# Placing the finest level's sums: half tiles of TensorE replaced by quarter tiles, twice as many

## The chip, the cores and the metric

The kernel runs on one core of one Trainium2 chip. The metric is the device time of one execution in microseconds, as the median of several runs. Beside it there is one profiled execution, whose trace gives every instruction's start and duration; its span is the time from its first to its last instruction. Both are given below.

## The reference

Two blocks follow each other. The first is a recurrent attention (RWKV6) with batch 4, 8 heads, 768 tokens and 48 channels a head; the second is a feed-forward layer with an exact GELU on the 3072 rows of 384 that come out of it.

```python
for t in range(S):
    kt, vt, rt, wt = (k[:, :, t], v[:, :, t], r[:, :, t], w[:, :, t])
    cur = np.einsum('bhd,bhe->bhde', u[None] * kt, vt)
    y[:, :, t] = np.einsum('bhd,bhde->bhe', rt, state + cur)
    state = wt[:, :, :, None] * state + np.einsum('bhd,bhe->bhde', kt, vt)
...
h = x @ w_in
g = 0.5 * h * (1.0 + erf(h / sqrt(2)))
out = g @ w_out
```

In chunks of 64 tokens the recurrence becomes a matrix of weights A between the tokens of a chunk (how much token i counts for the later token j: the sum over the channels of k, r and all decays w between them), times v, plus a term from the state before the chunk. All is 32-bit floating point.

## The kernel before

The work is cut into eight pieces x = 0 to 7 (batch element times half of the 768 tokens: 384 tokens each, C = 64 to a chunk). In a piece there are 4 pairs of heads. The two heads of a pair (g = 0, 1) lie in partitions 0 to 63 and 64 to 127 (48 of 64 rows are used). The six chunks of a pair are taken two at a time (p = 0, 1), so there are n_b = 12 units of two chunks of two heads in a piece. `a_sb` holds A: its partitions are the 128 tokens of the unit's two chunks, its columns the 64 tokens of the same chunk, for both heads and all 12 units.

Pieces 0 and 1 build A in `halves()` (line 492), by levels of doubling size. Pieces 2 to 7, six in all, build it in `quarters()` (line 563), by two levels of a factor of four, h = FINE = 4 and h = 16 (`QUARTERS`, loop at line 592), and what is finer than 4 tokens, the finest level, apart. The finest level is this: VectorE multiplies k and r token by token for all pairs of tokens (distance e = 0 to 3) within groups of four (`apart`, line 405, and line 414), and one VectorE instruction for each distance (`transposed_sums`, line 400) transposes them in blocks of 32 by 32 and adds them up over 32 channels. `fine_sb[row, e, a, n]` then holds, in row 32z + i, what the block z of 32 channels adds to the pair of tokens (4i + a, 4i + a + e) of unit n. Two such blocks z belong to a head.

What is left is to add the two blocks of a head and to bring the sum for token 4i + a to row 4i + a. TensorE does both, with `places` (made once, lines 304 to 309): a matrix of zeros and ones whose row 32z + i has its one in column 4i + a. Line 601 multiplies, for each a = 0 to 3 and each head g, the 64 rows of head g of `places` (stationary, 128 columns, hence a half tile of the array: 64 rows by 128 columns) by (4 - a) times 12 columns of `fine_sb` (48, 36, 24 and 12 columns), and adds the products up in the last 48 columns of the bank of PSUM that belongs to g (`fine_of`, line 615). That is 8 products a piece.

These products stand in `burst` (line 595), which issues the level's main products: line 609 multiplies, for each unit n, head g and chunk p, a 64 by 64 block of k by 96 columns of r laid out in `kx` (a quarter tile of the array: 64 rows by 64 columns). For h = FINE there are three bursts of 5, 5 and 2 units. The last one (`behind == n_b`) issues the 8 placing products first and then its own 8. Then come, on VectorE, line 663 (r of the next level), line 670 and line 674 (k of the next level, which may start only once the last burst has read k), lines 585 and 586 (laying out), the copies of the burst's blocks to `a_sb` under masks (line 642), and at last two masked copies of the finest level's sums from PSUM to `a_sb` (line 692), one for each head. ScalarE copies plain parts of r to `kx` (line 580) after the last burst. The level h = 16 repeats this without the finest level; in pieces 2, 3, 5 and 7 it issues its bursts in one go, and two tiles named `d` of two banks each go around between all bursts, so its first burst or its second waits until line 692 has read the tile of FINE's last burst. Later in a piece, lines 732 (k times v), 773 (A times v) and 818 (state times r) are quarter tiles too, with 48 and 64 columns.

All engines work through their queues in the order in which the program issues; no scheduler changes it. The order between the pieces is written by hand: `PLAN[x]` is a string in which each letter advances one stream by one step up to its next `yield`: "." the feed-forward layer of piece x - 1 (`mlp`, products at lines 950, 1076, 1090 and 1222 with full tiles of 128 by 128), "s" the attention of piece x, and others for loads and sums. So the bursts of piece x stand in TensorE's queue between the big products of piece x - 1, and ScalarE's GELUs and copies and VectorE's sums for that layer stand between the attention's steps.

In the trace every 32-bit product shows as two passes, each with a weight load (LDWEIGHTS) and a matmul (MATMUL) of its own.

Of the kernel before, what the change touches and what calls it, by code (L numbers as in the profile page):

```python
# [20 lines left out]
C = 64  # L21
# [9 lines left out]
FINE = 4  # L31
# [44 lines left out]
def kernel(  # L76
# [25 lines left out]
    nc = tc.nc  # L102
# [21 lines left out]
    def pair(name):  # L124
        return pools["d"].tile([128, 2, BANK], F32, name=name, tag="d")
# [9 lines left out]
    def bank_u(i):  # L135
        return pools["u"].tile([128, BANK], F32, name="u_ps", tag=f"u{i % 2}")
# [5 lines left out]
    half = [slice(0, 64), slice(64, 128)]  # L142
# [14 lines left out]
    fine_sb = bufs[0][:, SPARE:SPARE + FINE * FINE * NPART * NI].rearrange("p (e a n) -> p e a n", e=FINE, a=FINE)  # L157
    places = bufs[0][:, 3 * ALL - FINE * 128:].rearrange("p (a r) -> p a r", a=FINE)
# [217 lines left out]
    def attention(x, unit):  # L376
# [186 lines left out]
        def quarters():  # L563
# [27 lines left out]
            n_b = np_ * NI  # L591
            for h in QUARTERS:
                m, r4, t4, s0, s1, s2 = views(h)

                def burst(first, behind, spare=False):

                    d = [bank_u(i) for i in range(2)] if spare else pair("d")
                    if behind == n_b and h == FINE:
                        for a in range(FINE):
                            for g in range(2):  # L600
                                nc.tensor.matmul(fine_of(d, g)[:, a * n_b:], lhsT=places[half[g], a],  # L601
                                                 rhs=fine_sb[half[g], 0:FINE - a, a],
                                                 start=(a == 0), stop=True, skip_group_check=True)
                    for n in range(first, behind):
                        i = n - first
                        for g in range(2):
                            for p in range(2):
                                o = d[g] if isinstance(d, list) else d[:, g]
                                nc.tensor.matmul(o[half[p], i * 3 * C // 2:(i + 1) * 3 * C // 2],  # L609
                                                 lhsT=kc[half[g], n // NI, n % NI, p],  # L610
                                                 rhs=rx[half[g], 2 * n + p], start=not spare or i == 0, stop=True,
                                                 skip_group_check=True)
                    return d

                def fine_of(d, g):
                    return d[:, g, BANK - FINE * n_b:]
# [30 lines left out]
                cuts = (0, n_b // 3, 2 * n_b // 3, n_b) if whole else (0, 5, 10, n_b)  # L647
                parts_of = list(zip(cuts, cuts[1:]))
                ds = [burst(*parts_of[0])]
                if not whole:  # L650
                    yield
                ds.append(burst(*parts_of[1]))
                if whole:
                    ds.append(burst(*parts_of[2], spare=True))
# [67 lines left out]
        def vs(b, i, g):  # L722
            o = ((parts[b] * NI + i) * 2 + g) * D
            return loaded[x][1][:, o:o + G]

        kvs = []
        for b in range(np_):
            kv_ps = pair("kv_ps")
            for i in range(NI):
                for p in range(2):  # L730
                    for g in range(2):
                        nc.tensor.matmul(kv_ps[half[g], p, i * D:(i + 1) * D], lhsT=k_t(b, i, p, g),  # L732
                                         rhs=vs(b, i, g)[half[p], 0:D], start=True, stop=True)
# [74 lines left out]
        for i in range(NI):  # L808
            for p in range(2):
                for b in range(np_):  # L810
                    q, c3 = divmod(i, N3)
                    for g in range(2):
                        c = 2 * c3 + (p + g) % 2
                        src, c0 = (st, c - 1) if c else (before, NC - 1)
                        if src is None:
# [3 lines left out]
                                         lhsT=src[half[g], o:o + G], rhs=rc[half[g], b, i, c % 2],  # L819
                                         start=False, stop=True, skip_group_check=True)  # L820
# [525 lines left out]
```

## Time and profile before

| | |
|---|---|
| median of 3 runs | 598.23 us (598.77, 595.89, 598.23) |
| profiled execution, its own time | 597.41 us |
| its span | 595.6 us |
| TensorE clock granted, mean | 0.997 |
| passes of line 601 in the trace | 96, of 256 to 307 ns each as the profile models them |
| passes of line 609 in the trace | 1152, of 242 to 294 ns each |

The profile's durations of matmuls overlap: they are pipelined, and their ends are modelled. What a group of products costs TensorE is read from where it starts and where the next group starts. "PE" is TensorE's matmuls, "PEld" its weight loads, "DVE" VectorE, "ACT" ScalarE. A form such as 64*128 64x48 is a tile of 64 rows by 128 columns and a moving operand of 48 columns. In a timeline line the columns are the start in us from the span's start, how long the merged group lasts, the engine, the line of the kernel, the operation, what it writes and reads, and how many records it merges; in brackets, how long the engine had been idle and for whom it waited.

### The profile page before, as it was taken

Reading aid. Unit: us, or ns where it says so; the run is one execution under the profiler, and the core shown is the slowest. Engines: PE = TensorE matmul, PEld = TensorE weight load, DVE = VectorE, ACT = ScalarE, POOL = GpSimd, SP = SyncE. Lnnn points to the kernel's source line nnn. Section 1 sums busy time; section 2 is a strip of 40 time slices with the busy share of each in tenths; the row PEclk is TensorE's granted clock in tenths of the full one; section 3 lists DMA queues with packets and bytes.
Section 4 is the critical chain, followed back from the end, with each engine's and each line's share of the span. In section 5 each row is a group of like instructions: output and inputs, shape, how many; then the busy total and the mean of one; then the engine's idle time right before and its main releaser. Section 6 shows DMA issues by size and latency. Waiting matters only on the chain.

```text
span 595.6 us, 17175 instructions
## 1 busy us (share of the span) xinstructions
PE 577.2 (97%) x7410; PEld 511.3 (86%) x7424; DVE 447.2 (75%) x857; ACT 280.0 (47%) x647; POOL 8.0 (1%) x21
## 2 busy tenths in 40 slices
PE   5779999999999999999999999999999999999997
PEld 3566666656699999999999999999999999999997
DVE  5978989997868977798849977799858978631211
ACT  2258789313533645235652554335652454435500
POOL 3100000000000000000000000000000000000000
PEclk8999999999999999999999999999999999999999
DMA  7467753220141301431032310432022100310000
GB/s 235 137 221 284 263 180 110 75 69 1 19 131 49 125 2 18 127 120 38 1 63 89 106 50 8 115 103 76 3 40 79 62 1 2 68 32 0 1 14 27
DMA packets 50859, 46.79 MB, mean 79 GB/s; under 512 B 31712, under 2 KB 35936, under 8 KB 50784
## 3 DMA queue, kind: packets, MB, share of 16 engines
q1 hardware_dynamic: 50688, 45.62, 25.1%
q8 instruction: 58, 0.95, 0.6%
q14 instruction: 17, 0.14, 0.1%
q10 hardware_dynamic: 96, 0.07, 0.1%
HBM read 36.24 MB, written 4.72 MB: 69 GB/s over the span
## 4 chain that ended last, share of the span: by engine, by line
PE 92%; DMA 2%; DVE 2%; ACT 1%; issue 1%; SPq 0%; DVEq 0%; ACTq 0%
PE o_ps L1090 31%; PE h_ps L950 16%; PE u_ps L950 13%; PE h_ps L1076 10%; PE o_ps L1222 5%; PE d L609 4%; PE kv_ps L732 2%; PE y_ps L773 2%; PE y_ps L818 2%; PE d L475 2%; PE u_ps L1090 2%; DMA raw<-in_w_in_dram 1%; DMA rkw<-in_rkw_dram 1%; PE d L601 1%; DVE rkw L528 0%
## 5 line engine op out<-in xcount | busy, mean ns | idle before, releaser
L950 PE MATMUL h_ps<-xT,w_in_sb 128*128 128x192 f32 x480 | 95.0, 330 | 0.0
L950 PEld LDWEIGHTS h_ps<-xT,w_in_sb 128*128 128x128 f32 x480 | 79.7, 190 | 3.1 <-ACT g L982 1.4
L1076 PE MATMUL h_ps<-xT,w_in_sb 128*128 128x384 f32 x192 | 64.2, 490 | 0.4 <-ACT g L1079 0.4
L1076 PEld LDWEIGHTS h_ps<-xT,w_in_sb 128*128 128x128 f32 x192 | 35.8, 190 | 24.2 <-ACT g L1079 0.5
L1090 PE MATMUL o_ps<-w_out_sb,g 128*128 128x192 f32 x224 | 39.7, 326 | 0.0
L1090 PEld LDWEIGHTS o_ps<-w_out_sb,g 128*128 128x128 f32 x224 | 37.0, 190 | 0.3
L950 PE MATMUL u_ps<-s,w_in_sb 128*128 128x192 f32 x192 | 35.1, 326 | 0.0
L475 PEld LDWEIGHTS d<-rkw 64*64 64x64 f32 x1152 | 19.1, 137 | 15.6 <-issue 8.6
L1222 PE MATMUL o_ps<-w_out_sb,g 128*128 128x384 f32 x96 | 32.5, 491 | 0.0
L625 ACT COPY a_sb<-d 32x256 f32<-32x256 f32 (+8 forms) x84 | 30.5, 363 | 3.4 <-PE d L609 2.0
L642 DVE COPY_PREDICATED a_sb<-quarter,d 128x480 f32<-128x480 uint8 (+5 forms) x54 | 23.1, 438 | 11.9 <-PE d L609 10.6
L950 PEld LDWEIGHTS u_ps<-s,w_in_sb 128*128 128x128 f32 x192 | 31.9, 190 | 0.0
L1150 DVE TENSOR_TENSOR u<-o_ps,p 128x192 f32<-128x192 f32 x7 | 2.5, 357 | 37.3 <-PE o_ps L1090 37.3
L1090 PE MATMUL o_ps<-w_out_sb,f 128*128 128x192 f32 x160 | 29.4, 331 | 0.0
L747 DVE SCALAR_TENSOR_TENSOR st<-st,tot_sb,kv_ps 128x48 f32<-128x48 f32 x160 | 28.8, 256 | 0.2 <-PE kv_ps L732 0.2
L475 PE MATMUL d<-rkw 64*64 64x64 f32 (+1 forms) x1152 | 21.5, 224 | 7.7 <-DMA rkw<-in_rkw_dram 3.7
L1090 PE MATMUL o_ps<-t,g 128*128 128x192 f32 x160 | 28.6, 330 | 0.0
L1004 DVE TENSOR_TENSOR g<-g,o_sb 128x384 f32<-128x384 f32 x24 | 13.1, 547 | 20.4 <-ACT o_sb L986 20.4
L1090 PE MATMUL o_ps<-w_out_sb,e 128*128 128x192 f32 x160 | 28.4, 329 | 0.0
L1090 PE MATMUL o_ps<-t,e 128*128 128x192 f32 x160 | 28.0, 327 | 0.0
L1090 PE MATMUL o_ps<-t,s 128*128 128x192 f32 x160 | 27.7, 327 | 0.0
L1222 PEld LDWEIGHTS o_ps<-w_out_sb,g 128*128 128x128 f32 x96 | 17.7, 190 | 11.4
(170 smaller groups left out, 1195.2 us busy)
## 6 DMA issues: line engine op xcount, KB each, us to landing
rkw<-in_rkw_dram SPq DMA_DIRECT2D x54, 256.0 KB, 3.7
raw<-in_w_out_dram SPq DMA_DIRECT2D x8, 768.0 KB, 4.5
v_in<-in_v_dram SPq DMA_DIRECT2D x8, 584.0 KB, 4.3
raw<-in_w_in_dram SPq DMA_DIRECT2D x5, 768.0 KB, 6.4
out_dram<-o_sb SPq DMA_DIRECT2D x20, 192.0 KB, 2.0
rkw<-kx SPq DMA_DIRECT2D x72, 48.0 KB, 2.1
rkw<-in_rkw_dram SPq DMA_DIRECT2D x6, 384.0 KB, 6.6
raw<-in_w_in_dram SPq DMA_DIRECT2D x9, 256.0 KB, 4.8
```

The lines of the kernel that those rows point to most:

```text
L475: nc.tensor.matmul(d[half[p], g, n * width:(n + 1) * width], lhsT=kc[half[g], b, i, p], rhs=right(half[g], b, i, p), start=True, stop=True)
L609: nc.tensor.matmul(o[half[p], i * 3 * C // 2:(i + 1) * 3 * C // 2], lhsT=kc[half[g], n // NI, n % NI, p], rhs=rx[half[g], 2 * n + p], star ...
L625: nc.scalar.copy(out=at[z, g, first:behind, (a + 1) * h:], in_=d[z, :, :, to] if g == slice(None) else d[z, :, to])
L642: nc.vector.copy_predicated(out=an[:, :, :, :, (a + 1) * h:], mask=mask.to_broadcast(data.shape), data=data)
L732: nc.tensor.matmul(kv_ps[half[g], p, i * D:(i + 1) * D], lhsT=k_t(b, i, p, g), rhs=vs(b, i, g)[half[p], 0:D], start=True, stop=True)
L747: nc.vector.scalar_tensor_tensor(out=stq[:, q, c], in0=stq[:, q, c - 1] if c else b4[:, q, NC - 1], scalar=totq[:, q, c:c + 1], in1=kvs[q ...
L773: nc.tensor.matmul(y[p][half[g ^ swap(b)], i * C:(i + 1) * C], lhsT=vs(b, i, g)[half[p]], rhs=at[half[p], g, b * NI + i, :], start=(i == 0 ...
L950: nc.tensor.matmul(o, lhsT=lhsT, rhs=rhs, start=start, stop=True, skip_group_check=True)
L1004: nc.vector.tensor_add(g_of(q, 0, 1), g_of(q, 0, 1), z)
L1076: nc.tensor.matmul(h_ps, lhsT=w_in_sb[:, f // FI, j, f % FI * 128:(f % FI + 1) * 128], rhs=xT[:, j, :], start=(j == 0), stop=(j == NJ - 1))
L1090: nc.tensor.matmul(o, lhsT=lhs(j), rhs=rhs(j), start=start and j == 0, stop=(j == HF - 1), skip_group_check=True)
L1222: nc.tensor.matmul(o, lhsT=block(i, f // HF, f % HF), rhs=w_out_sb[:, f, :], start=(f == 0), stop=(f == NF - 1))
```

## The change

Each placing product is cut into two, one for each chunk p: 64 of the 128 columns of `places` as the stationary operand, into the 64 partitions of the output that belong to p. The moving operand is the same for both. There are 16 products a piece on quarter tiles in place of 8 on half tiles, and what lies in PSUM afterwards is the same. Nothing else is changed: no other engine's instructions, no buffers, and not the order of the work.

```diff
                     if behind == n_b and h == FINE:
                         for a in range(FINE):
                             for g in range(2):
-                                nc.tensor.matmul(fine_of(d, g)[:, a * n_b:], lhsT=places[half[g], a],
-                                                 rhs=fine_sb[half[g], 0:FINE - a, a],
-                                                 start=(a == 0), stop=True, skip_group_check=True)
+                                for p in range(2):
+                                    nc.tensor.matmul(fine_of(d, g)[half[p], a * n_b:],
+                                                     lhsT=places[half[g], a, p * C:(p + 1) * C],
+                                                     rhs=fine_sb[half[g], 0:FINE - a, a],
+                                                     start=(a == 0), stop=True, skip_group_check=True)
```

## The prediction

> **What bounds the kernel now.** I read the page's busy times and its chain first, then the chain in order of time around one change site, then the timeline of that site, then the timelines of other quarter-tile products for their price, and last who waits for whom.
>
> ```profile
> PE 577.2 (97%) x7410; PEld 511.3 (86%) x7424; DVE 447.2 (75%) x857; ACT 280.0 (47%) x647; POOL 8.0 (1%) x21
> ...
> PE 92%; DMA 2%; DVE 2%; ACT 1%; issue 1%; SPq 0%; DVEq 0%; ACTq 0%
> ```
>
> TensorE is busy for 97% of the span, and 92% of the chain that ended last is TensorE. The chain in order of time shows the same around the placing products of piece 3: TensorE passes from big products to L601, to L609, and back, and nothing else is in between.
>
> ```profile
> 210.90 2.15 PE h_ps L950 x12
> 213.05 0.99 PE d L601 x16
> 214.04 0.49 PE d L609 x16
> 214.54 1.50 PE u_ps L950 x8
> ```
>
> So what TensorE saves here is time off the end, unless a wait grows. The timeline of TensorE at the first site (piece 2) gives the price of today's form; start times are what count, since the durations overlap.
>
> ```profile
> 143.18 1.06 PE L601 MATMUL d<-rkw 64*128 64x48 f32 x16
> 144.18 0.56 PE L609 MATMUL d<-kx,rkw 64*64 64x96 f32 x16
> 144.66 0.59 PE L1076 MATMUL h_ps<-xT,w_in_sb 128*128 128x384 f32 x1
> ```
>
> The 16 half-tile passes take 1.00 us (143.18 to 144.18), 62 ns each; the 16 quarter-tile passes behind them take 0.48 us, 30 ns each, though they move 96 columns and not 12 to 48. The starts of the single records show more: half-tile passes come in rounds of two (the two heads, 7 ns apart), a round every 112 ns whether it moves 48 or 12 columns. Between the last half-tile round (143.98) and the first quarter-tile pass (144.18) lie 186 ns.
>
> **What the Trainium skill says.** "TensorE: Matmul & The Clock Gate", section "LDWEIGHTS (loading the stationary operand)": a weight load takes the number of its columns divided by 1.2, in ns, and the number of rows doesn't matter. For 128 columns that is 107 ns, for 64 it is 53 ns. The trace agrees: a round every 112 ns on half tiles, and in L818 (64 columns of weights, 64 moving) a round of four passes every 58 to 59 ns. "TensorEngine Tiling (Array Packing)", section "Key Properties": changing the tiling mode, not merely the tile, drains TensorE, while different tiles load and multiply in parallel. The trace agrees with both: 186 ns at the change from half to quarter tiles against 112 ns within, and four quarter tiles starting 7 ns apart. The first page, under "Wait — 56ns, not 53.3ns?", also gives a floor of about 25 ns between the starts of matmuls, however small. This trace differs, with 15 ns a pass on quarter tiles (next part), so the measurement decides.
>
> **The change part by part.** Per piece it removes 16 half-tile passes and adds 32 quarter-tile passes, in six pieces (96 records of L601 divided by 16). It also removes one change of mode: big products, half tiles, quarter tiles, big products becomes big products, quarter tiles, big products.
>
> *Before, per piece:* from the first L601 to the next big product, 143.18 to 144.66, 1.48 us (1.485 from the single starts; the five other sites, by their single starts, lie within 3 ns of it).
>
> *The price of a quarter-tile pass with few columns* comes from two stretches of L818 that differ only in length:
>
> ```profile
> 179.18 1.39 PE L818 MATMUL y_ps<-rkw,st 64*64 64x64 f32 x80
> 180.50 0.43 PE L1090 MATMUL o_ps<-t,s 128*128 128x192 f32 x1
> ```
>
> ```profile
> 254.49 1.63 PE L818 MATMUL y_ps<-rkw,st 64*64 64x64 f32 x96
> 256.05 0.43 PE L1090 MATMUL o_ps<-w_out_sb,f 128*128 128x192 f32 x1
> ```
>
> 80 passes take 1.32 us up to the next big product and 96 take 1.56 us. The 16 more cost 0.23 us (unrounded), 14.6 ns each; what does not grow with the number, entering and leaving the mode, is 1.325 - 80 x 0.0146 = 0.155 us. L732 with 48 columns (96 passes in 1.545 us) and L475 with 32 (96 in 1.53 us) give the same: below 64 columns the number doesn't count, so the 48 to 12 columns here are priced at 14.6 ns too. With 96 columns it does: 80 passes of L609 take 1.81 us, 16 take 0.49 us, so 20.6 ns each.
>
> *After, per piece:* one stretch in one mode: 0.155 + 32 x 0.0146 + 16 x 0.0206 = 0.155 + 0.467 + 0.330 = 0.95 us. Saved: 1.485 - 0.95 = 0.535 us. Six pieces: 3.2 us. This is all on the path: at no site but two does TensorE wait before L601, and there for 0.2 us only, for VectorE's copy L642 of a burst that was issued earlier; that wait stays.
>
> *Bounds of the unknown cost.* The trace has no quarter-tile pass that moves 12 columns, nor one that adds onto a sum three products in a row. From below in gain: the price of L609's pass, 20.6 ns, gives 0.155 + 0.659 + 0.330 = 1.14 us, a gain of 0.34 us, 2.1 us in six. From above: nothing but the loads, 53 ns for a round of four, 13.3 ns a pass (an estimate from the page on TensorE), gives 0.91 us, a gain of 0.575 us, 3.4 us in six. I take 14.6 ns, since three lines of different width agree on it.
>
> *The other engines* get no instruction more. What waits for the last burst comes sooner: VectorE's L670 and ScalarE's L580.
>
> ```profile
> 282.56 0.96 DVE L670 TENSOR_TENSOR rkw<-rkw,tot_sb 128x768 f32<-128x768 f32 x1 [0.52 <-PE d L609]
> 282.60 1.34 ACT L580 COPY kx<-rkw 128x384 f32<-128x384 f32 x3 [1.29 <-PE d L609]
> ```
>
> In pieces 2, 4 and 6 VectorE stands idle for 0.72, 0.52 and 0.51 us before L670 until L609 is through, so it moves forward with TensorE, by all or nearly all of the 0.535 us. In pieces 3, 5 and 7 L670 does not wait, as VectorE is still at L663 when L609 ends. There VectorE does not move, and TensorE comes 0.535 us nearer to it.
>
> *What is late next.* In pieces 4 and 6 the second burst of h = 16 already waits about 0.17 us for L692 to free its `d` (80 passes from 289.76 take 1.98 us where elsewhere they take 1.81). VectorE gains 0.51 to 0.52 us there, TensorE 0.535: the wait grows by 0.02 us, nothing. In piece 7 the last L692 ends at 498.03 and the burst that needs it, after the change of mode (256 ns from the last big product), starts at 499.07: a cover of 0.8 us or more against 0.535 us. In piece 3 the last L692 ends near 223.5 and the burst starts at 226.4: a cover of over 2 us. If piece 7's cover were gone, up to 0.535 us would be lost, once. The big products behind the site take banks that ScalarE freed microseconds earlier, and the engine that would have to keep up is only 47% busy.
>
> **The sum.** 6 x 0.535 = 3.2 us off the profiled execution: span 595.6 to 592.4, its own time 597.41 to 594.2. That execution lies 0.8 us below the median of the runs, so the forecast for the median is 598.23 - 3.2 = 595.0 us, 0.54% less. The three runs lie 2.9 us apart, so one median may be off by a microsecond or so. About 0.5% (3.0 us) is what a measurement of this kernel can tell from no change.
>
> **The rivals.**
>
> *Part of the gain is taken back by VectorE.* In pieces 3, 5 and 7, where L670 does not wait, TensorE arrives earlier at something VectorE has not finished, and loses all it won there: three pieces remain, 1.6 us, 596.6 us. For it: VectorE is 75% busy and back to back for some ten microseconds behind these sites. Against it: the covers above, and no wait of TensorE over 0.2 us in these pieces between the site and the next burst.
>
> *The rounds keep their 112 ns.* If a round is paced not by the load but by adding onto the sum that the pass before it wrote on the same tile, 8 rounds of four take as long as 8 rounds of two, and only the change of mode is saved, about 0.12 us a piece: 0.7 us, 597.5 us. For it: today's rounds are alike for 48 and 12 columns. Against it: in L818 each second pass also adds onto the first, every 59 ns.
>
> *A pass has a fixed price (slower).* If what sets the 62 ns of a half-tile pass is issue and not the columns loaded, 32 passes cost 1.98 us: 1.98 + 0.155 + 0.33 = 2.47 us a piece against 1.485, or 5.9 us in six: 604.1 us. It decides from 31 ns a pass on ((1.485 - 0.485) / 32), and from 47 ns by over 0.5%. For it: twice the instructions a piece, each of which has to be issued. Against it: L818, L732, L475 at 15 ns and L609 at 21 ns, right behind L601.
>
> **How the numbers follow.** Full gain, 595.0 us: 0.74 (with its bounds and the runs' scatter 593 to 596.5). VectorE takes part of it, 596.6 us: 0.16. Rounds keep their pace, 597.5 us: 0.05. Fixed price, 604.1 us: 0.05. The range 592.8 to 597.4 holds the first two cases with their scatter and part of the third. Faster by over 0.5% means below 595.2 us: the first case lies just beyond that bound (0.72 of it), and a tenth of the second with good scatter: 0.55. Slower: the fourth, and a little scatter: 0.07. The rest, 0.38, is within 0.5%.
>
> **What would show it.** In the profile after: 192 records of the placing line, of form 64*64; the stretch from the first of them to the next big product 0.95 us, not 1.48; rounds of four every 58 to 59 ns; no gap between the placing line and the line of the burst beyond a round. L670 waits shorter in pieces 2, 4 and 6. Wrong would be a stretch of 1.3 us or more (rounds, or a price per pass), or the stretch shortened with a new wait of TensorE for L692 or ScalarE behind it.

## The result and the profile after

The changed kernel takes 595.26 us (median of 22 runs, 591.66 to 598.64), the kernel before 597.03 us in the same sessions (22 runs, 595.23 to 602.32). The medians lie 1.8 us apart, the means 2.5. The ratio of the runs is 0.9959, with a 95% interval from 0.994 to 0.9977: 0.41% less, or 2.4 us, with 1.4 and 3.6 us as the ends. The forecast of 0.54% less lies inside, and so does 3.2 us. The profiled execution took 595.17 us, with a span of 593.4 us.

The page's busy times, TensorE first (busy time, share of the span, records):

```profile
PE 576.5 (97%) x7506; PEld 510.4 (86%) x7520; DVE 446.9 (75%) x857; ACT 279.2 (47%) x647; POOL 8.0 (1%) x21
```

There are 96 passes more on TensorE and as many instructions as before on the other engines. In the chain in order of time around the site of piece 3 (start, duration, what), the placing products (now line 602) and the burst (now line 611) still follow each other on TensorE alone:

```profile
211.06 2.15 PE h_ps L952 x12
213.21 0.58 PE d L602 x32
213.79 0.38 PE d L611 x16
214.16 1.50 PE u_ps L952 x8
```

TensorE's timeline at the first site, piece 2:

```profile
143.87 0.65 PE L602 MATMUL d<-rkw 64*64 64x48 f32 x32
144.35 0.54 PE L611 MATMUL d<-kx,rkw 64*64 64x96 f32 x16
144.82 0.59 PE L1078 MATMUL h_ps<-xT,w_in_sb 128*128 128x384 f32 x1
```

From the first placing pass to the next big product, a stretch that is called a site from here on, it is 0.96 us where it was 1.48. By the single starts the six sites take 957 or 958 ns each, against 1485 or 1486 before: 5.75 us in all against 8.92, so 3.17 us saved. The step from the last big product into a site is as before to within 4 ns. The 32 passes start within 449 ns, in rounds of four. The first three rounds are 93, 59 and 44 ns apart, the others 58 to 59; before, rounds of two were 146, 112 and 97 ns apart and then 112. The burst follows after 38 or 39 ns instead of 186 (after 9 or 10 in pieces 4 and 6, where one of the four tiles runs some 30 ns ahead of the others).

VectorE and ScalarE at the site of piece 4, where both waited for the burst before (0.52 and 1.29 us):

```profile
281.57 0.96 DVE L672 TENSOR_TENSOR rkw<-rkw,tot_sb 128x768 f32<-128x768 f32 x1
281.71 1.34 ACT L580 COPY kx<-rkw 128x384 f32<-128x384 f32 x3 [0.85 <-DVE rkw L665]
```

VectorE no longer waits there, and ScalarE waits for VectorE. In piece 2 VectorE's wait fell from 0.72 to 0.19 us.

### The profile page after: what moved, and what is told of

Same layout as the page of the kernel before. It is cut to its first block, busy times and chain, and to the rows that moved or that the text cites. A ratio compares the mean times of both kernels' runs of the same rounds, so it can differ in the third digit from the quotient of the medians.

```text
span 593.4 us, 17367 instructions
## 1 busy us (share of the span) xinstructions
PE 576.5 (97%) x7506; PEld 510.4 (86%) x7520; DVE 446.9 (75%) x857; ACT 279.2 (47%) x647; POOL 8.0 (1%) x21
## 4 chain that ended last, share of the span: by engine, by line
PE 93%; DVE 2%; DMA 2%; ACT 2%; issue 1%; SPq 0%; DVEq 0%; ACTq 0%
PE o_ps L1092 31%; PE h_ps L952 16%; PE u_ps L952 13%; PE h_ps L1078 10%; PE o_ps L1224 5%; PE d L611 4%; PE d L475 2%; PE y_ps L775 2%; PE kv_ps L734 2%; PE y_ps L820 2%; PE u_ps L1092 2%; DMA rkw<-in_rkw_dram 1%; DVE rkw L528 1%; ACT a_sb L536 1%; DMA raw<-in_w_in_dram 1%
```

## The experiments

A single time scatters by several us, so what a kernel does at the six sites is read from its trace, to the nanosecond. Where the end of the kernel is the question, runs are timed against the kernel before, or the stretch is taken from the first big product of piece 1's feed-forward layer to the end, which leaves the loads at the start out.

**Half tiles, eight times over**

```diff
-                        for a in range(FINE):
+                        for a in 8 * list(range(FINE)):
```

> The eight placing products of a piece on half tiles, as before, issued eight times over (the first product of each set starts the sum afresh, so the result stays). Theory, the columns loaded set the pace: seven more sets of 8 rounds at 112 ns are 0.896 us each, 6.27 us a piece, 37.6 us in six pieces, so 634.6 us against 597.0. Rival, a fixed price of issue per pass: the same here, it is the run with quarter tiles that tells. If VectorE or ScalarE covered part of it, less than 37.6 us.

**Quarter tiles, eight times over**: the same edit in the changed kernel.

> The sixteen placing products on quarter tiles, issued eight times over. Theory: seven more sets of 8 rounds of four at 58.5 ns are 0.468 us each, 3.28 us a piece, 19.7 us in six, so 595.0 + 19.7 = 614.7 us, about 20 us below the run with half tiles eight times over. Rival, rounds keep 112 ns: 632 us. Rival, a fixed price of 62 ns a pass: 595 + 83 us. If the end of the kernel doesn't follow TensorE in full, the gain in time over the half tiles is smaller than the gain in the sites' own length.

Measured: 664.64 us for half tiles (ratio 1.1082, 1.0993 to 1.1171) and 631.23 us for quarter tiles (1.0524, 1.0458 to 1.0589). Both theories' numbers were missed, by 30 and by 17 us. A part of that is the start: the kernel before, run beside them, took 601.35 us, where the theories reckoned with 597.0. The rest is that such long stretches meet limits that the real ones do not. For half tiles, the table by stretches of time has the granted clock ("PEclk", 1.00 is full) behind the engines' busy times:

```profile
core 0: us, PE busy (x) PEld busy (x) DVE busy (x) ACT busy (x) POOL busy (x), PEclk, DMA share, GB/s
143.40:147.00 3.60, 3.60 (x67) 3.60 (x66) 0.88 (x1) 0.55 (x2) 0.00 (x0) 1.00 0.00 0
148.40:153.40 5.00, 5.00 (x58) 4.81 (x56) 0.00 (x0) 0.00 (x0) 0.00 (x0) 0.50 0.00 0
154.30:158.60 4.30, 4.30 (x8) 2.32 (x7) 4.09 (x8) 1.19 (x4) 0.00 (x0) 0.50 0.00 0
```

After 5.0 us of placing passes the clock fell to half, though TensorE never stood idle, and the big products behind ran at half clock too, up to 158.6. The rounds show the same: every 112 ns at first, every 213 ns from there on. It happened at all six sites, 3.1 to 6.0 us into the stretch. For quarter tiles the clock fell at two sites (pieces 4 and 7), and at all six TensorE stopped once, after 134 to 228 passes, with nothing to wait for that the profile shows; here in piece 3:

```profile
218.73 3.12 PE L602 MATMUL d<-rkw 64*64 64x48 f32 x199
222.76 1.01 PE L602 MATMUL d<-rkw 64*64 64x48 f32 x57 [0.91 <-issue]
```

The six stops are 1.1 to 1.7 us from one start to the next, 8.5 us in all. What remains of the two runs is the pace at full clock: in the mean rounds of two half tiles at 112 ns and rounds of four quarter tiles at 58 to 59 ns, set after set. That is the theory's price; 62 ns a pass and rounds of four at 112 ns are refuted. As measures of what the end gains, the two runs are of no use.

**Half tiles twice**: the same edit with 2 in place of 8, to stay below these limits.

> The placing products on half tiles as before, issued twice. A stretch of 1.9 us of them, shorter than the 3 us and more after which the clock fell when they were issued eight times. Theory: one more set of 8 rounds at 112 ns, 0.896 us a piece, 5.4 us in six, 602.4 us against 597.0 (0.9% more), the clock full. Rival, the other engines hide part of it: less than 3 us. If the clock falls already here, more than 6 us.

Measured: 602.61 us against 598.25 for the kernel before on the same chip, ratio 1.0085 (1.0059 to 1.0111), so 5.1 us more (3.5 to 6.6). The clock granted was 1.0 in its profile. The sites grew by 5.36 us in all (14.27 against 8.92). Nothing hides part of it: what TensorE does here counts in full, within the interval.

**The first quarter-tile products alone**

```diff
-                        for a in range(FINE):
+                        for a in range(1):
```

> Of the placing products on quarter tiles only those of a = 0 are issued; those of a = 1, 2 and 3 are left out, and with them most of the finest level's sums. Theory, TensorE's queue sets the end and no other engine is close behind: 6 of 8 rounds of 58.5 ns go, 0.35 us a piece, 2.1 us in six, beyond the changed kernel: 595.3 - 2.1 = 593.2 us, or 5.3 us (0.9%) below before. Rival, VectorE takes back what TensorE gains: its waits appear in pieces 3, 5 and 7 and the time stays near 595 us.

Measured: 592.98 us against 598.25, ratio 0.9921 (0.9901 to 0.9941), 4.7 us less (3.5 to 5.9) where 5.3 were expected. The sites take 3.65 us in all, 5.27 less than before. VectorE takes a little back, but in pieces 4 and 6 and not in 3, 5 and 7. TensorE and VectorE in piece 4:

```profile
286.68 1.92 DVE L694 COPY_PREDICATED a_sb<-fine_mask,d 128x768 f32<-128x768 uint8 x2
...
287.39 1.06 PE L611 MATMUL d<-kx,rkw 64*64 64x96 f32 x40
...
288.65 1.06 PE L611 MATMUL d<-kx,rkw 64*64 64x96 f32 x40 [0.20 <-DVE a_sb L694]
```

In the changed kernel the 80 passes were one group:

```profile
288.79 2.05 PE L611 MATMUL d<-kx,rkw 64*64 64x96 f32 x80
```

Now their second half waits for line 694 to free its tile. Against the changed kernel the wait grew by 0.26 us there and by 0.29 in piece 6. The theory holds up to here, and the next limit is in sight: VectorE's copies in pieces 4 and 6, which take 0.55 us back from a gain of 5.27.

**Half tiles for two, quarter tiles for two**

```diff
-                        for a in range(FINE):
+                        for a in range(2):
 ...
+                        for a in range(2, FINE):
+                            for g in range(2):
+                                for p in range(2):
 ...
```

> The placing products of a = 0 and 1 on half tiles, those of a = 2 and 3 on quarter tiles: half of the rounds are shortened, and the number of changes of mode is that of before. Theory: the rounds give 4 x 53.5 = 0.21 us, the saved change of mode gives the other 0.1 us only when all are quarter tiles; the site is 1.485 - 0.214 = 1.27 us. If the saved change of mode is nothing and the rounds give all, half of the 0.527 us is saved: 1.22 us. If a change within the placing products costs more than one before the burst: over 1.27 us.

TensorE's timeline at the first site:

```profile
144.66 0.64 PE L601 MATMUL d<-rkw 64*128 64x48 f32 x8
145.23 0.42 PE L607 MATMUL d<-rkw 64*64 64x24 f32 x16
145.49 0.54 PE L616 MATMUL d<-kx,rkw 64*64 64x96 f32 x16
145.96 0.59 PE L1083 MATMUL h_ps<-xT,w_in_sb 128*128 128x384 f32 x1
```

The site takes 1.29 us (1292 ns at five sites, 1293 at one), 0.02 over the 1.27 of the theory. The step from half to quarter tiles lies at 206 ns between two starts, where it was 186 before the burst: the 0.02. So four shortened rounds save 0.21 us, eight 0.43, and the 0.527 us of the whole change leave 0.10 us for the change of mode that went. Without this working, as measured, the first half of the products saves 0.19 us, and the second half, with which the change of mode goes, 0.33. In one execution it took 597.89 us.

**All of chunk 0 first, then all of chunk 1**

```diff
-                        for a in range(FINE):
-                            for g in range(2):
-                                for p in range(2):
+                        for p in range(2):
+                            for a in range(FINE):
+                                for g in range(2):
```

> The sixteen quarter-tile products in another order, all of chunk 0 first and then all of chunk 1, so that only two tiles follow each other before the first comes again. Theory (a tile's round lasts as long as its 64 columns load, and the gain of quarter tiles is that four tiles load at once): 16 rounds of two at 58 ns, 0.93 us, site 0.95 + 0.46 = 1.42 us, nearly all of the gain gone. Rival (a quarter-tile pass costs 14.6 ns whatever tile it goes to): site 0.96 us, as in the changed kernel.

```profile
142.46 0.74 PE L602 MATMUL d<-rkw 64*64 64x48 f32 x26
142.99 0.29 PE L611 MATMUL d<-kx,rkw 64*64 64x96 f32 x1
143.03 0.26 PE L602 MATMUL d<-rkw 64*64 64x24 f32 x3
...
143.67 0.59 PE L1078 MATMUL h_ps<-xT,w_in_sb 128*128 128x384 f32 x1
```

The site takes 1.21 us, between the two: of the gain of 0.527 us, 0.25 are lost by the order alone. The instructions are the same, so a pass has no price of its own; it depends on how many tiles are at work. A tile's own pace does not: as long as only the two tiles of chunk 0 were at work, their rounds were 94, 58, 44 and 58 ns apart, as those of four tiles are in the changed kernel. But it is not rounds of two throughout either. The single starts show the first passes of chunk 1 (48 columns) 0.27 us after the site's start, beside the passes of chunk 0 with 24 columns, and passes of line 611 before the last ones of line 602, which stand ahead of them in the program. So a pass on a free tile overtakes those that wait for their tile. Both times six earlier passes had not yet started when the first of the later ones did. In one execution it took 595.08 us.

**Tiles of 32 columns**

```diff
-                                for p in range(2):
-                                    nc.tensor.matmul(fine_of(d, g)[half[p], a * n_b:],
-                                                     lhsT=places[half[g], a, p * C:(p + 1) * C],
+                                for p in range(4):
+                                    nc.tensor.matmul(fine_of(d, g)[p * 32:(p + 1) * 32, a * n_b:],
+                                                     lhsT=places[half[g], a, p * 32:(p + 1) * 32],
```

> The placing products cut once more, to tiles of 64 rows by 32 columns, 32 products and 64 passes a piece. Theory 1, the load of the columns sets the pace: 32 columns are 27 ns, rounds of eight every 32 ns, 8 rounds 0.26 us, but a change of mode before the burst comes back (0.1 us): site about 0.85 us. Theory 2, the starts 7 ns apart are a limit of issue: eight starts are 56 ns, 8 rounds 0.45 us and the change of mode: site about 1.06 us. A fixed 14.6 ns a pass: 64 passes 0.93 us, site 1.5 us.

```profile
213.48 0.77 PE L602 MATMUL d<-rkw 64*32 64x48 f32 x64
214.18 0.56 PE L611 MATMUL d<-kx,rkw 64*64 64x96 f32 x16
214.67 0.43 PE L952 MATMUL u_ps<-s,s_home 128*128 128x192 f32 x1
```

The site takes 1.19 us (1.175 in pieces 4 and 6), 0.23 more than with quarter tiles. The load of 32 columns is not what sets the pace: the first 32 passes start 6 ns apart on average, the other 32 10.8 ns apart (335 ns), and the change of mode is back. Theory 2 is nearest, and it is 0.13 us short; what sets the pace of the second half stays open. Cutting further does not pay here.

**Placing products among the burst's own**: those of a = 0 and 1 first, then a unit of the burst, a = 2, the other unit, a = 3.

```diff
+                    if fine:
+                        place(0)
+                        place(1)
                     for n in range(first, behind):
 ...
-                                                 rhs=rx[half[g], 2 * n + p], start=not spare or i == 0, stop=True,
+                                                 rhs=rx[half[g], 2 * n + p], start=not fine and (not spare or i == 0), stop=True,
 ...
+                        if fine and i < 2:
+                            place(2 + i)
```

The products of that burst also lose their flag `start` here.

> The quarter-tile placing products of a = 2 and 3 are issued between and behind the burst's own products instead of all ahead of them; nothing is left out. If on a tile the next pass is loaded while the one before it streams, and a pass costs the larger of the two, the order doesn't matter and the site stays at 0.96 us. If loads can run further ahead than one pass, the loads of the placing passes hide under the 96 columns: down to 0.87 us. If changing between long and short passes costs something: over 0.96 us.

```profile
212.35 0.44 PE L603 MATMUL d<-rkw 64*64 64x48 f32 x16
212.61 0.38 PE L616 MATMUL d<-kx,rkw 64*64 64x96 f32 x8
212.80 0.26 PE L603 MATMUL d<-rkw 64*64 64x24 f32 x8
212.89 0.37 PE L616 MATMUL d<-kx,rkw 64*64 64x96 f32 x8
213.08 0.25 PE L603 MATMUL d<-rkw 64*64 64x12 f32 x8
213.26 0.43 PE L959 MATMUL u_ps<-s,s_home 128*128 128x192 f32 x1
```

The site takes 0.91 us, 0.05 less than in the changed kernel: the second round behind a unit of the burst starts 28 ns after the first, not 58. That lies half-way between the first expectation and the second. It is the shortest of all, but 0.27 us in six pieces is below what the time of the kernel can tell (one execution, 594.0 us).

**A stop of 0.3 us: the changed kernel three times more, and the kernel before again.** In the profile of the changed kernel TensorE stopped once for 0.3 us within the state products of piece 5, which took 1.9 us up to the next big product, where 96 such passes elsewhere take 1.56:

```profile
388.60 1.98 PE L820 MATMUL y_ps<-rkw,st 64*64 64x64 f32 x96
390.52 1.57 PE L1092 MATMUL o_ps<-w_out_sb,f 128*128 128x192 f32 x8
```

> The changed kernel once more, for one thing: in its profile TensorE stood still for 0.3 us within the 96 passes of the state products of piece 5, with nothing to wait for that the profile shows, and the kernel before did not. If this belongs to the changed stream of instructions it stands at the same place again; if it is chance it is gone or elsewhere.

> The same, once more: a stop of 0.3 us in the state products of piece 5 in all three profiles if the stream of instructions makes it, otherwise not.

Of the three, the last has 64 tiny products more at its start:

```diff
+    t = ps.tile([128, BANK], F32, name="warm", tag="mm", bufs=2)
+    for _ in range(64):
+        nc.tensor.matmul(t[0:32, 0:8], lhsT=zeros[:, 0:32], rhs=zeros[:, 0:8], start=True, stop=True)
```

> The changed kernel with 64 tiny products (8 columns of zeros) more at its start, where TensorE waits for the first loads: they shift all later instructions by 128, half of what one transfer of instructions brings (16 KB, at 64 bytes 256 of them), so that at piece 5 the stream stands to the transfers as before the change. If the stop comes from where in the stream a transfer falls, it is gone from piece 5, or elsewhere; if it belongs to the state products' own data or to chance, the shift has nothing to do with it.

> The kernel before once more, for a second profile. Theory: from the first product of the feed-forward layer of piece 1 (at 125.60 us in the first profile) to the end it takes within 0.2 us of the 470.0 us of that profile, about 3.1 us more than the changed kernel's three profiles, whatever the time up to there. Rival: the stretch scatters by a microsecond as the whole does, and then the difference of 3.1 us in it says little.

They took 594.62, 598.67, 596.99 and, the kernel before, 597.55 us. The 64 bytes of the expectation come out of the trace of the changed kernel: 59 transfers of instructions, 0.97 MB in all, for TensorE's 7506 passes and 7520 loads. In the first repetition the state products of piece 5 take 1.56 us, with no stop. In the second they take 1.68, a stop of 0.12 us at the same place, and so they do in the kernel with half tiles twice. The shifted kernel has no stop there, but one of 0.8 us among the products of k and v in piece 5 and one of 0.2 us in piece 2; the kernel before, repeated, stops for 0.3 us among the products of k and v. So such stops come with half tiles and quarter tiles alike, and the one of 0.3 us is not the change's. What causes them stays open. The stretch from the first big product of piece 1's layer to the end, from the traces' starts (us):

| kernel | starts at | to the end | of it the six sites | all else |
|---|---|---|---|---|
| before | 125.60 | 469.99 | 8.92 | 461.07 |
| before again | 125.20 | 470.55 | 8.92 | 461.64 |
| changed | 126.28 | 467.10 | 5.75 | 461.35 |
| changed, again | 126.10 | 466.73 | 5.75 | 460.99 |
| changed, third | 129.98 | 466.87 | 5.75 | 461.13 |
| changed, shifted | 127.51 | 467.69 | 5.75 | 461.95 |
| half tiles twice | 125.78 | 475.43 | 14.27 | 461.15 |
| a = 0 alone | 125.83 | 465.62 | 3.65 | 461.98 |

The expectation of 0.2 us was too narrow, since the two profiles of before lie 0.56 apart, but the two kernels are clear of each other: 470.3 against 466.9 us in the mean of the first two rows and of the next three, 3.4 us, of which 3.17 are the sites. The last column says more: the sites go from 3.65 to 14.27 us, and all else stays at 461.0 to 462.0. So it does in the mixed kernel, the one with chunk 0 first, the one with 32 columns and the one with the products in between (461.1 to 461.3). The two highest values are the kernel with a stop of 0.8 us and the one whose waits for VectorE grew by 0.55. So the end follows the sites' length in full. The start of the stretch moves by 4.8 us between executions of the two kernels, and the whole time with it: the 598.67 us of "changed, third" are a late start, not a slow rest.

## Why the prediction was right, point by point

*What bounds it.* Right. The chain is TensorE's, before and after (92 and 93% of it). Doubling the half tiles cost the end 5.1 us (3.5 to 6.6) for 5.36 us at the sites, leaving three quarters of the quarter-tile products out gave 4.7 (3.5 to 5.9) for 5.27, and the change 2.4 (1.4 to 3.6) for 3.17. In the stretch that leaves the start out it is 3.4 for 3.17, and all else in it is the same to within a microsecond.

*The price of a pass.* 14.6 ns from the state products, and 14.5 ns measured (449 ns over 31 steps). The whole site was put at 0.95 us and took 0.958. Apart from the first three rounds, the widths of 48 to 12 columns did not matter, nor did adding onto the same sum. The rounds on half tiles, which the prediction called alike, differ at the start in the same way.

*The change of mode.* It was put into the 0.155 us of entering and leaving, counted once in place of twice. With the mixed kernel it comes out at about 0.10 us of the 0.527.

*What the Trainium skill says.* The rule of "TensorE: Matmul & The Clock Gate", section "LDWEIGHTS (loading the stationary operand)", held for 128 and 64 columns, with rounds of 112 and 58 to 59 ns. For 32 columns it gives 27 ns as an estimate, and there it no longer sets the pace. The drain at a change of mode ("TensorEngine Tiling (Array Packing)", section "Key Properties") shows as 186 to 206 ns between two starts, where two rounds of half tiles just before are 112 or less apart.

*What is late next.* Right for pieces 4 and 6: the second burst of the next level waits 0.17 and 0.16 us, as before. It was right to look for VectorE, but the rival's place, pieces 3, 5 and 7, was wrong: even with three quarters of the placing products gone it is pieces 4 and 6 that wait.

*The size of the end's gain.* The sum said 3.2 us; the sites give 3.17, and the timed runs say 2.4 with 3.2 inside their interval. That the middle is lower is not explained by a new wait in any of three profiles; the time up to 125 us, which moves by microseconds between executions, is enough for it, but that it is the cause is argued and not shown. That the forecast of 595.0 us lies 0.3 us from the measured 595.26 is in part luck: it stands on a median of three runs, 598.23 us, which 22 runs put at 597.03, and the medians fell by 1.8 us and not by 3.2, so two deviations nearly cancel. And 0.41% falls short of the 0.5% that the prediction thought it likelier than not (0.55) to exceed.

*The rivals.* A fixed price and unshortened rounds are refuted by the site's length. VectorE taking back half the gain is refuted by the traces, in which no wait of TensorE for another engine between these sites and the end grows by more than some 0.02 us, and by the last column of the table.

## What to carry to other kernels

The cost of a product on TensorE that moves few columns (12 to 64 here) went with its stationary columns: a tile took its next pass after 112 ns with 128 of them, after 58 to 59 with 64. So two products on two tiles of half the width took about half the time of one wide one, as long as neighbours in the program went to different tiles. It does not go on like this: with tiles of 32 columns the site was longer than with 64. Put such products beside others of the same tile shape, as a change from half to quarter tiles cost about 0.1 us here. When a kernel's time scatters more than the effect, read the effect at its site in the trace and test with a doubled dose whether the end follows; keep the dose small enough that it meets no other limit.

## What the runs showed that was not expected

- TensorE's clock fell to half in a stretch of narrow passes without an idle moment, 3.1 to 6.0 us after its start on half tiles, and the big products behind ran at half clock for some microseconds. The Trainium skill, "TensorE: Matmul & The Clock Gate", Part 1, says that the gate watches how busy TensorE is; here a gapless stretch with 12 to 48 moving columns a pass didn't keep the clock up. What the gate counts in place of it was not tested. With sites of 0.6 to 2.4 us, in all the other kernels, the clock stayed full there.
- Passes on free quarter tiles start ahead of earlier ones in the program that wait for their tile: in the kernel with all of chunk 0 first, the burst's first pass started 0.17 us before the last placing pass. That engines work through their queues in the order of the program, as said at the start, holds for TensorE only up to such steps.
- With quarter tiles eight times over, 134 to 228 passes (each with its load, so up to 456 instructions) ended in a stop of 1.1 to 1.7 us at every site. Transfers of instructions (three, 0.05 MB in 10 us around that of piece 3) run beside it, and at each of the six sites one of them lands within 0.5 us of the stop's start. That TensorE ran out of instructions fits, but was not tested.
